# Seven block products in one more batch, all folds in one batch, and an order without a table of shifts

## The chip, the cores and the metric

The kernel runs on one core of a Trainium2 chip. The metric is the device time of one execution, in microseconds; less is better.

## The reference

Attention with a memory of 32 slots, then a two-layer perceptron with a squared ReLU, all in fp32:

```python
a = softmax(phi, axis=sequence)                  # phi: 8 batches, 8 heads, 576 x 32
k_m = einsum('bhsm,bhsd->bhmd', a, k)            # 32 x 64 for each head
v_m = einsum('bhsm,bhsd->bhmd', a, v)
attn = softmax(q @ k_m.T / 8, axis=slots) @ v_m  # 576 x 64 for each head
x = attn, with heads joined                      # 4608 x 512
h = x @ w_in                                     # 512 x 2048
g = relu(h) ** 2
out = g @ w_out                                  # 2048 x 512
```

## The kernel before, in words

**Products.** Each fp32 operand of a large product is split into a rounded part and a rest (hi and lo), and three matmuls stand for one: hi x hi, hi x lo, lo x hi. v_m is never multiplied with the attention weights: it is folded into w_in beforehand (vw_alone, vw_step and vw_quad), so that the first product of the perceptron takes the attention weights (ath, atl: 256 x 576 for a batch) and a folded w_in (tiles vw).

**Stages.** memory(b, hh), a "unit", makes k_m and v_m of four heads of a batch. attention(b) makes scores (psc, line 840), the softmax (lines 949 to 955) and the turned weights at, ath and atl (lines 971 to 975). Then a batch has 16 steps, one for each 128 columns of w_in: mm1(g) (line 1013, into the banks h, then relu and square into gh and glo) and mm2(g) (lines 1044, 1045, 1047, into four banks acc, 512 columns each, one for each 128 tokens). g counts steps: batch b, from 2 on, has 16b to 16b + 15. The last 64 tokens of each batch go into tiles gl, and are multiplied for two batches at once (mm2_left, accl, line 1279).

**Folds of batches 4 to 7.** vw_quad(s, hh) folds one piece of w_in for all four batches at once: twelve matmuls into the banks pv and pa (pvq, line 784), ScalarE's cast (line 412, the line of the helper that copies), VectorE's subtraction (line 791), and POOL's store to DRAM (vw_kept, line 794). All use one buffer, named fold. Eight pieces s, two halves hh each; WHEN says after which steps of batches 3 and 4 a piece is recorded. vw_again loads the folded tiles back (line 805).

**Seven block products.** In batches from FAST on, fast(b, t, s) replaces mm1 and mm2: two steps' blocks of g (2 x 2 blocks with the 128-token blocks) and w_out are combined into sums, so that seven products of 256 columns do the work of eight. Its mm1 is line 1151, the sums are made on VectorE (lines 1171 to 1174), split into tiles H (ScalarE, line 1179) and LA, LB (VectorE, line 1180), and multiplied at lines 1208, 1209 and 1211 into banks Ma to Md. combine(s) turns w_out in place into the sums that these products need, during the batch before FAST. fast_left is what mm2_left is for these batches.

**What sets the order.** Every instruction is recorded as an Op of Plan with a cost and its dependences. Plan.order derives a due time for each and runs a list scheduler forward (and backward for due times), some twenty times; each engine takes the ready op with the smallest key. Before the last run a table, MOVED, shifts keys: a task (an invocation of a function, cut into pieces of 12 ops by named, begin and PART) gets its number times 100 ns added. TensorE's queue then runs in the order so found; where no op is ready for long in the first part, filled puts in filler matmuls.

Of the kernel before, what the change touches and what calls it, by code (L numbers as in the profile page):

```python
# [48 lines left out]
}  # L49
# [1425 lines left out]
```

## Time and profile before

| what | value |
| --- | --- |
| three runs | 762.48, 765.95, 766.16 us (median 765.95) |
| the profiled execution | 761.47 us, its span 759.4 us |
| TensorE's granted clock | 0.999 |
| busy: TensorE, VectorE, ScalarE | 739.4, 606.0, 414.0 us |
| DMA | 135.62 MB, mean 179 GB/s |

Steps begin at 44.0 us (batch 0), 248.3 (batch 2), 331.1 (batch 3), 437.2 (batch 4), 522.7 (batch 5), 592.8 (batch 6) and 670.7 (batch 7). The span goes from the first to the last instruction, and the time of an execution is about 2 us more. PE is TensorE, PEld its weight loads (beside the matmuls), DVE is VectorE, ACT is ScalarE. Records of neighbouring matmuls overlap, so what one costs is read from rows of several in a row, not from its own length. The granted clock of 0.999 is the upper of TensorE's two levels, 2.4 GHz, all the time.

### The profile page before, as it was taken

To read this page: it belongs to the slowest core of one execution; us is meant where nothing else is said; L and a number is where in the kernel's file an instruction comes from. 1 tells how busy PE (TensorE), PEld (TensorE's weight loads), DVE (VectorE), ACT (ScalarE), POOL (GpSimd) and SP (SyncE) were. 2 spreads that over 40 slices of the span, in tenths; PEclk is the share of its full clock that TensorE was granted. 3 is DMA by queue.
4 is the path that set the end of the run, shared out by engine and by line. 5 is a ranking of instruction groups with operands and counts; after the bars stand their busy time and mean duration, and the time that the engine had idled before them with its cause. 6 is when DMAs were issued, how large, how long until landed. Compare 5 with 4: busy or idle time off the path is not lost.

```text
span 759.4 us, 14838 instructions
## 1 busy us (share of the span) xinstructions
PE 739.4 (97%) x5392; PEld 648.5 (85%) x5392; DVE 606.0 (80%) x1410; ACT 414.0 (55%) x928; POOL 77.8 (10%) x133
## 2 busy tenths in 40 slices
PE   4999999999999999999999999999999999999997
PEld 3687889888787888888888888888888999999997
DVE  4899999996679799867478546578999878987984
ACT  3577788875462565633344223435675745755561
POOL 4112221110100100001101211101000100000000
PEclk9999999999999999999999999999999999999999
DMA  9998996667755947634667878764310345445421
GB/s 268 315 303 227 286 288 202 190 193 201 212 144 170 249 135 208 189 107 122 220 203 247 267 201 273 257 181 106 110 32 0 90 115 149 139 131 160 137 76 42
DMA packets 82632, 135.62 MB, mean 179 GB/s; under 512 B 26080, under 2 KB 52704, under 8 KB 82560
## 3 DMA queue, kind: packets, MB, share of 16 engines
q1 hardware_dynamic: 67168, 98.40, 44.9%
q0 software_dynamic: 15296, 36.15, 15.9%
q8 instruction: 43, 0.70, 0.4%
q14 instruction: 29, 0.24, 0.1%
q10 hardware_dynamic: 96, 0.13, 0.1%
HBM read 96.14 MB, written 34.80 MB: 172 GB/s over the span
## 4 chain that ended last, share of the span: by engine, by line
PE 84%; DVE 7%; DMA 5%; issue 2%; ACT 1%; SPq 1%; POOL 0%; DVEq 0%; POOLq 0%; ACTq 0%
PE h L1013 18%; PE acc L1047 11%; PE acc L1044 11%; PE acc L1045 11%; PE h L1151 6%; PE accl L1263 3%; PE psc L840 3%; PE accl L1279 3%; PE pkv L622 2%; PE pvw L754 2%; PE pvq_pv L784 2%; DMA vw<-vw_kept 1%; DVE work L500 1%; PE Mc L1211 1%; DMA wi<-w_in_kept 1%
## 5 line engine op out<-in xcount | busy, mean ns | idle before, releaser
L1013 PE MATMUL h<-ath,vw 128*128 128x256 f32 (+1 forms) x768 | 157.5, 301 | 0.0
L1044 PE MATMUL acc<-wo,gh 128*128 128x512 f32 x384 | 155.1, 404 | 0.0
L1045 PE MATMUL acc<-wo,gh 128*128 128x512 f32 x384 | 150.9, 393 | 0.0
L1013 PEld LDWEIGHTS h<-ath,vw 128*128 128x128 f32 x768 | 124.9, 189 | 10.2 <-ACT r L1017 0.7
L1047 PE MATMUL acc<-wo,glo 128*128 128x512 f32 x384 | 127.4, 402 | 0.0
L1017 ACT ACTIVATE r<-h 128x320 f32<-128x320 f32 (+1 forms) x136 | 54.2, 406 | 61.5 <-PE h L1013 56.3
L1019 ACT ACTIVATE gh<-r 128x512 fp32r<-128x512 f32 x96 | 60.6, 632 | 45.2 <-DVE r L1018 23.3
L1044 PEld LDWEIGHTS acc<-wo,gh 128*128 128x128 f32 x384 | 72.3, 188 | 14.3 <-issue 0.4
L1047 PEld LDWEIGHTS acc<-wo,glo 128*128 128x128 f32 x384 | 70.7, 188 | 16.0 <-issue 0.8
L1045 PEld LDWEIGHTS acc<-wo,gh 128*128 128x128 f32 x384 | 72.3, 188 | 12.5
L1013 PE MATMUL h<-atl,vw 128*128 128x256 f32 (+1 forms) x384 | 82.4, 295 | 0.1
L1023 DVE TENSOR_TENSOR glo<-r,gh 128x512 fp32r<-128x512 f32 x96 | 65.7, 685 | 15.3 <-PE acc L1047 8.0
L1013 PEld LDWEIGHTS h<-atl,vw 128*128 128x128 f32 x384 | 61.6, 189 | 0.5 <-DVE atl L935 0.3
L1021 ACT ACTIVATE r<-r 128x576 f32<-128x576 f32 x77 | 52.7, 684 | 1.8
L1151 PE MATMUL h<-ath,vw 128*128 128x256 f32 (+1 forms) x256 | 52.9, 299 | 0.4 <-DMA vw<-vw_kept 0.3
L412 ACT CAST vw<-pvw 64x512 fp32r<-64x512 f32 (+1 forms) x64 | 37.1, 580 | 22.7 <-PE pvw L754 16.9
L1018 DVE TENSOR_SCALAR r<-h 128x320 f32<-128x320 f32 (+1 forms) x56 | 25.6, 457 | 27.4 <-PE h L1013 26.6
L1151 PEld LDWEIGHTS h<-ath,vw 128*128 128x128 f32 x256 | 39.8, 188 | 1.5 <-issue 0.7
L762 DVE TENSOR_TENSOR vw<-pvw,vw 64x512 fp32r<-64x512 f32 x48 | 33.0, 687 | 4.5 <-ACT vw L412 3.6
L794 POOL DMA_DIRECT2D vw_kept<-fold x32 | 17.3, 540 | 108.0 <-DVE fold L791 100.2
L598 DVE TENSOR_REDUCE mx<-phi 128x128 f32<-128x640 f32 x16 | 21.1, 1316 | 8.7 <-DMA phi<-in_phi_dram 6.4
L840 PE MATMUL psc<-qT,kb 128*128 128x256 f32 (+1 forms) x96 | 27.4, 407 | 0.3 <-DVE qT L835 0.3
(254 smaller groups left out, 1614.4 us busy)
## 6 DMA issues: line engine op xcount, KB each, us to landing
vw<-vw_kept SPq DMA_DIRECT2D x192, 128.0 KB, 4.3
wi<-w_in_kept SPq DMA_DIRECT2D x40, 512.0 KB, 4.8
vw_kept<-fold POOLq DMA_DIRECT2D x32, 512.0 KB, 4.2
KV<-in_v_dram SPq DMA_DIRECT2D x16, 512.0 KB, 6.4
...
```

Of the source, the lines that this page charges most:

```text
L412: nc.scalar.copy(o, i) if e == "ACT" else ENG[e].tensor_copy(o, i)
L762: vec({"DVE": 700}, lambda e, part=part, pr=pr: nc.vector.tensor_sub(part(1), pw()[pr], part(0).bitcast(F32)), [pw, (V, (0, hf))], [(V, (1 ...
L840: nc.tensor.matmul(pq()[:, 0:32 * n], kb()[:, x].rearrange("p h m -> p (h m)"), qT()[:, x, 0:n].rearrange("p c t -> p (c t)"), start=(x == ...
L1013: nc.tensor.matmul(p()[:, 0:n], V()[:, l, hh, c0:c0 + P], x()[:, hh, cs], start=(i == 0), stop=(i == 5))
L1017: op({"ACT": act(n) - 40, **({} if b < 2 else {"DVE": tt(n)})}, lambda e, cs=cs, n=n, p=p: nc.scalar.activation(r()[:, cs], p()[:, 0:n], A ...
L1019: op({"ACT": act(SM)}, lambda e: nc.scalar.activation(gh(), r()[:, 0:SM], AF.Square), [r], [gh])
L1021: op({"ACT": act(S), **({} if b < 2 or b == FAST - 1 else {"DVE": tt(S)})}, lambda e: nc.scalar.activation(r(), r(), AF.Square) if e == "A ...
L1023: vec({"DVE": tt(SM)}, lambda e: nc.vector.tensor_sub(glo(), r()[:, 0:SM], gh().bitcast(F32)), [r, gh], [glo])
L1044: nc.tensor.matmul(a(), gh()[:, c], t()[:, 0], start=f0, stop=False)
L1045: nc.tensor.matmul(a(), gh()[:, c], t()[:, 1], start=False, stop=False)
L1047: nc.tensor.matmul(a(), glo()[:, c], t()[:, 0], start=False, stop=f1)
L1151: nc.tensor.matmul(p()[:, at:at + n], V()[:, l, hh, f0:f0 + P], x()[:, hh, cs], start=(i == 0), stop=(i == 5))
```

## The change

Batch 5 is done with seven block products too (FAST 6 to 5), so combine runs in batch 4. All eight pieces of the folds of batches 4 to 7 are recorded in batch 3, and none in batch 4. The units of batches 4 to 7 come earlier: seven in batch 2 and one in batch 3, where there were four and four. The second half of each fold goes into two buffers of the tag vw0. The table of shifts is removed, with what numbered its tasks. The buffers for the last ordinary batch's output come in another order.

```diff
-PART = 12
-MOVED = {
-    1: -263, 2: -101, 6: 20, 10: 21, 18: 27, 20: 61, 22: -57, 28: -6, 32: 388, 36: 21, 42: 15, 52: -266, 54: 53,
...
-}
...
-    def begin(self):
...
-    def named(self, fn):
...
-        if self.steps == PART:
-            self.begin()
-        self.steps += 1
         o = Op()
-        o.task = self.task
...
-        moved = [k + 100 * MOVED.get(o.task, 0) for k, o in zip(best[1], self.ops)]
-        self.forward(moved)
+        self.forward(best[1])
...
-    FAST = 6
+    FAST = 5
...
-    @plan.named
     def decode(kind, j, h, room):
...
-    WHEN = (8, 10, 12, 14), (0, 3, 6, 9)
-
-    @plan.named
+    WHEN = (3,5,6,8,9,11,13,15),()
+
     def vw_quad(s, hh):
 
         if not room:
             room.append(st([P, 2, 2, 2, SL], F32R, "KV", "fold"))
-        Z = room[0]
+        if hh:
+            Z = [(st([P, 2, 2, SL], F32R, "vw0", f"fold{s}_{g}", 2), None) for g in (0, 1)]
+        else:
+            Z = [(room[0], g) for g in (0, 1)]
...
         for g in (0, 1):
-            part = lambda l, g=g: Z()[:, g, l].rearrange("p x f -> p (x f)")
...
+            z, i = Z[g]
+            view = lambda z=z, i=i: z() if i is None else z()[:, i]
+            part = lambda l, view=view: view()[:, l].rearrange("p x f -> p (x f)")
...
         if b == FAST - 1:
-            return [(st([P, DM], F32, x, f"o{b}_{i}", n), None) for i, (x, n) in enumerate((("r", 2), ("r", 2), ("qT", 1), ("S", 2)))]
+            return [(st([P, DM], F32, x, f"o{b}_{i}", n), None) for i, (x, n) in enumerate((("qT", 1), ("S", 2), ("r", 2), ("r", 2)))]
...
+    ready = []
+
     def quad(s):
...
-        if s in (1, 2, 6, 7):
+        if s in (0, 1, 2, 3, 5, 6, 7):
             units(1)
     for ff in range(NFF):
         step(pos[3, ff])
-        if ff < 8 and ff % 2 == 0:
+        if ff in (0,):
             units(1)
         if ff in WHEN[0]:
             quad(WHEN[0].index(ff))
...
-            if b == FAST - 1 and ff % 2:
-                combine(ff // 2)
+            if b == FAST - 1 and ff % 2 and (b > QUAD or ff > max(WHEN[1], default=-1)):
+                for s in range(len(ready), ff // 2 + 1):
+                    ready.append(combine(s))
```

Behind the cut, line numbers are lower by 40 to 52: line 784 becomes 740, 791 becomes 749, 840 becomes 796, 1013 becomes 966, 1023 becomes 976, 1044 and 1045 become 996 and 997, 1180 becomes 1130, 1279 becomes 1227.

**TensorE, the last score product of batch 4** (psc4_1_1; acc3 and gh58 or gh63 are mm2 of batch 3; accl3 is mm2_left). Before, it stood in step 58:

```order
L1044 MATMUL acc3_0_0_4347<-wo50_1609,gh58_4837 128x512
L1045 MATMUL acc3_0_0_4347<-wo50_1609,gh58_4837 128x512
L840 MATMUL psc4_1_1_4869<-qT4_1_1_4853,kb4_1_3577 128x320 x2
L1044 MATMUL acc3_0_1_4354<-wo50_1609,gh58_4837 128x512
L1045 MATMUL acc3_0_1_4354<-wo50_1609,gh58_4837 128x512
```

Now it stands in step 63, and mm2_left and the last folds follow it:

```order
L996 MATMUL acc3_0_3_4356<-wo71_2099,gh63_5189 128x512
L997 MATMUL acc3_0_3_4356<-wo71_2099,gh63_5189 128x512
L796 MATMUL psc4_1_1_5296<-qT4_1_1_5282,kb4_1_3901 128x320 x2
L1227 MATMUL accl3_5231<-wo51_1661,gl2_5_3961 128x512 x3
L1227 MATMUL accl3_5231<-wo60_1916,gl2_6_4052 128x512 x3
L740 MATMUL pvq6_0_pv_5312<-wi2_6_0_5024,VTh21_3028 128x256
```

And at the end of this stretch, the last rows of the last half fold and the first matmuls of batch 4 (h64_0):

```order
L740 MATMUL pvq7_0_pa_5393<-wi2_7_0_5159,VTh21_3028 128x256
L740 MATMUL pvq7_0_pv_5391<-wi2_7_0_5159,VTl21_3038 128x256
L740 MATMUL pvq7_0_pa_5393<-wi2_7_0_5159,VTl21_3038 128x256
L966 MATMUL h64_0_5409<-ath4_5259,vw4_0_4564 128x256 x2
L966 MATMUL h64_0_5409<-atl4_5264,vw4_0_4564 128x256 x2
```

Before, five steps of batch 3 and six half folds stood between; now 18 matmuls of 512 columns and three half folds.

**VectorE, the same place: what it does from the copy of batch 3's output (o3) to atl4, the operand of h64_0.** S4_1 is the score tile of batch 4's second half, fold the tiles of vw_quad. Now:

```order
L371 COPY o3_0_5221<-acc3_0_1_4346 128x512
L749 TENSOR_TENSOR fold_4492<-pvq6_0_pv_5312,fold_4492 128x512
L907 TENSOR_REDUCE rz4_1_None_5344<-S4_1_5289 128x18
L749 TENSOR_TENSOR fold_4492<-pvq6_0_pa_5314,fold_4492 128x512
L908 TENSOR_SCALAR rz4_1_None_5344<-rz4_1_None_5344 128x18
L791 STREAM_TRANSPOSE qT5_0_0_5356<-q5_0_5291 128x2x256
L909 RECIPROCAL rz4_1_None_5344<-rz4_1_None_5344 128x18
L910 TENSOR_TENSOR S4_1_5289<-S4_1_5289,rz4_1_None_5344 128x576
L925 STREAM_TRANSPOSE at4_1_0_5380<-S4_1_5289 128x256
L749 TENSOR_TENSOR fold6_0_5378<-pvq6_1_pv_5360,fold6_0_5378 128x512
L749 TENSOR_TENSOR fold6_1_5382<-pvq6_1_pa_5362,fold6_1_5382 128x512
L929 TENSOR_TENSOR atl4_5264<-at4_1_0_5380,ath4_5259 128x256
```

Before, the same softmax stood among the steps of batch 3 (r60, glo59 further on):

```order
L844 STREAM_TRANSPOSE S4_1_4857<-psc4_1_1_4869 128x320
L828 TENSOR_TENSOR kb5_1_4883<-kTa5_1_3816,bd_72 128x256
L949 TENSOR_REDUCE red4_1_None_4887<-S4_1_4857 128x18
L950 TENSOR_TENSOR S4_1_4857<-S4_1_4857,red4_1_None_4887 128x576
L791 TENSOR_TENSOR fold_4535<-pvq2_0_pa_4893,fold_4535 128x512
L791 TENSOR_TENSOR fold_4535<-pvq2_0_pv_4891,fold_4535 128x512
L952 TENSOR_REDUCE rz4_1_None_4932<-S4_1_4857 128x18
L835 STREAM_TRANSPOSE qT5_0_0_4951<-q5_0_4860 128x2x256
L953 TENSOR_SCALAR rz4_1_None_4932<-rz4_1_None_4932 128x18
L954 RECIPROCAL rz4_1_None_4932<-rz4_1_None_4932 128x18
L955 TENSOR_TENSOR S4_1_4857<-S4_1_4857,rz4_1_None_4932 128x576
L1018 TENSOR_SCALAR r60_4977<-h60_1_4957 128x320
```

Ahead of the piece of now stand the same four instructions with which the piece of before begins (lines 844 to 950 there).

**VectorE, the start of batch 5** (glo79 is the last subtraction of batch 4's steps). Now, with the last pieces of combine (wo, T, E, F) and the sums of the first products (X, XD, LA):

```order
L976 TENSOR_TENSOR glo79_6273<-r79_6209,gh79_6243 128x512
L1046 TENSOR_TENSOR wo61_1900<-E6_1_6239,wo61_1900 128x256
L1046 TENSOR_TENSOR T6_6271<-F6_6041,T6_6271 128x512
L1051 TENSOR_TENSOR E7_1_6292<-F7_6198 128x256 x2
L1121 TENSOR_TENSOR X80_6252<-X80_6252,XD_6280 128x256
L1122 TENSOR_TENSOR X80_6252<-XD_6280,X80_6252 128x128
L1046 TENSOR_TENSOR wo70_2177<-E7_1_6292,wo70_2177 128x256
L1123 TENSOR_TENSOR XD_6280<-X80_6252 128x128
L1046 TENSOR_TENSOR wo71_2099<-E7_1_6292,wo71_2099 128x256
L1124 TENSOR_TENSOR XD_6280<-XD_6280 128x128
L1105 TENSOR_SCALAR X81_6324<-h81_0_6245 128x256
L1052 TENSOR_TENSOR F7_6198<-F7_6198 128x512
```

Before, with the output of batch 4 (o4) and ordinary steps (r80, r81, glo80):

```order
L1023 TENSOR_TENSOR glo79_6127<-r79_6083,gh79_6108 128x512
L971 STREAM_TRANSPOSE at5_1_1_6132<-S5_1_5984 128x320
L1024 TENSOR_TENSOR gl4_7_6062<-r79_6083,gl4_7_6062 128x64
L975 TENSOR_TENSOR atl5_5997<-at5_1_1_6132,ath5_5994 128x320
L412 COPY o4_0_6145<-acc4_0_0_5346 128x512
L412 COPY o4_1_6153<-acc4_0_2_5353 128x512
L835 STREAM_TRANSPOSE qT6_0_1_6165<-q6_0_5986 128x640
L844 STREAM_TRANSPOSE S6_0_6177<-psc6_0_0_6150 128x256
L1018 TENSOR_SCALAR r80_6174<-h80_1_6167 128x320
L1018 TENSOR_SCALAR r81_6196<-h81_0_6181 128x256
L844 STREAM_TRANSPOSE S6_0_6177<-psc6_0_1_6191 128x320
L1023 TENSOR_TENSOR glo80_6208<-r80_6174,gh80_6194 128x512
```

In the first steps of the program the order differs too: on VectorE, ahead of glo6, the subtraction of step 6, stand seven more instructions than before, and ahead of glo7 nine fewer.

## Rows read from the trace of the kernel before

**Rows 1.** The profile's page, its part 1: busy time of each engine, its share of the span, and instructions.
```profile
PE 739.4 (97%) x5392; PEld 648.5 (85%) x5392; DVE 606.0 (80%) x1410; ACT 414.0 (55%) x928; POOL 77.8 (10%) x133
```

**Rows 2.** Waits of TensorE between 183 and 760 us: who waited at which line, for whom: us in total, times, longest. The answer has one more row, of 0.2 us.
```profile
PE h L1151 <- DMA vw<-vw_kept: 0.3, 1, 0.3
PE psc L840 <- DVE qT L835: 0.3, 1, 0.3
...
```

**Rows 3.** Busy time in three stretches: first half of batch 0, batch 5, batch 6. Columns: us, then busy us (x instructions) of PE, of PE's weight loads, of DVE, ACT and POOL, granted clock, DMA share, GB/s.
```profile
44.00:101.90 57.90, 55.27 (x450) 46.77 (x449) 57.19 (x129) 45.28 (x99) 11.84 (x14) 1.00 0.92 270
522.70:592.80 70.10, 70.10 (x386) 61.66 (x385) 64.36 (x148) 45.12 (x105) 2.59 (x4) 1.00 0.22 55
592.80:670.70 77.90, 77.30 (x596) 75.36 (x595) 66.16 (x192) 47.65 (x118) 4.01 (x6) 1.00 0.50 134
```

**Rows 4.** The chain of waits, in order of time: start us, us, what. Rows of 512 columns (L1279), 256 (the first L1151, and L1263) and 320 (the second L1151).
```profile
233.37 4.15 PE accl L1279 x18
...
592.97 1.42 PE h L1151 x12
...
652.85 1.76 PE h L1151 x12
...
744.90 10.03 PE accl L1263 x84
```

**Rows 5.** Timeline of TensorE around one half of a fold of batches 4 to 7 (twelve matmuls of L784): start us, us, what. First matmul of it, and what follows it.
```profile
363.55 0.38 PE L784 MATMUL pvq_pv<-wi,VTh 64*128 64x256 f32 x1
...
364.45 0.50 PE L1013 MATMUL h<-ath,vw 128*128 128x256 f32 x2
```

**Rows 6.** Groups of VectorE's instructions, shapes apart: line, operation, out<-in, out<-in (partitions x elements), count | busy us, mean ns of one | idle us ahead of them. In the order in which the prediction adds them up.
```profile
L844 DVE STREAM_TRANSPOSE S<-psc 128x320 f32<-128x320 f32 x12 | 6.2, 513 | 3.6 <-PE psc L840 3.4
L828 DVE TENSOR_TENSOR kb<-kTa,bd 128x256 f32<-128x256 f32 x6 | 2.4, 394 | 0.0
L949 DVE TENSOR_REDUCE red_None<-S 128x18 f32<-128x576 f32 x12 | 9.0, 748 | 0.0
L950 DVE TENSOR_TENSOR S<-S,red_None 128x576 f32<-128x576 f32 x12 | 9.0, 751 | 0.2
L412 DVE COPY o<-acc 128x512 f32<-128x512 f32 x12 | 8.0, 688 | 2.5 <-PE acc L1047 2.2
L791 DVE TENSOR_TENSOR fold<-pvq_pv,fold 128x512 fp32r<-128x512 f32 x16 | 10.8, 678 | 1.4 <-ACT fold L412 1.4
L952 DVE TENSOR_REDUCE rz_None<-S 128x18 f32<-128x576 f32 x12 | 8.9, 742 | 1.2 <-ACT S L951 1.1
L791 DVE TENSOR_TENSOR fold<-pvq_pa,fold 128x512 fp32r<-128x512 f32 x16 | 11.0, 686 | 10.5 <-ACT fold L412 10.5
L953 DVE TENSOR_SCALAR rz_None<-rz_None 128x18 f32<-128x18 f32 x12 | 1.9, 162 | 0.1
L835 DVE STREAM_TRANSPOSE qT<-q 128x512 f32<-128x512 f32 x12 | 8.4, 701 | 2.1 <-DMA q<-in_q_dram 2.1
L954 DVE RECIPROCAL rz_None<-rz_None 128x18 f32<-128x18 f32 x12 | 3.2, 263 | 0.3
L955 DVE TENSOR_TENSOR S<-S,rz_None 128x576 f32<-128x576 f32 x12 | 9.1, 756 | 0.2
L971 DVE STREAM_TRANSPOSE at<-S 128x256 f32<-128x256 f32 x12 | 5.2, 437 | 0.1
L975 DVE TENSOR_TENSOR atl<-at,ath 128x256 fp32r<-128x256 f32 x12 | 5.0, 420 | 0.2
```

**Rows 7.** Timeline of VectorE at two neighbours: start us, us, what.
```profile
12.89 0.41 DVE L497 TENSOR_SCALAR work<-raw 128x512 f32<-128x512 f32 x1
13.23 0.42 DVE L499 TENSOR_SCALAR work<-raw 128x512 uint32<-128x512 uint32 x1
```

**Rows 8.** Busy time of the score matmuls alone (line 840), batch 5: us, PE busy (x records), PEld busy, granted clock, DMA share, GB/s.
```profile
522.70:592.80 70.10, 3.87 (x14) 2.08 (x12) 1.00 0.22 55
```

**Rows 9.** Waits of VectorE in batch 6 (592.8 to 670.7 us): us in total, times, longest.
```profile
DVE XD L1155 <- PE h L1151: 1.8, 4, 0.9
DVE qT L835 <- DMA q<-in_q_dram: 1.7, 1, 1.7
DVE LA L1180 <- ACT S L951: 1.2, 1, 1.2
DVE X L1171 <- ACT XD L1169: 0.8, 2, 0.5
```

**Rows 10.** Groups of VectorE's instructions, as in rows 6: two of the six passes that decode a weight piece.
```profile
L500 DVE SCALAR_TENSOR_TENSOR work<-work 128x512 uint32<-128x512 uint32 x32 | 22.0, 686 | 1.5 <-ACT work L498 1.4
L497 DVE TENSOR_SCALAR work<-raw 128x512 f32<-128x512 f32 x32 | 13.4, 419 | 1.0 <-DMA raw<-in_moe_w_in_dram 0.8
```

**Rows 11.** Busy time from the first to the last fold matmul, and in ten microseconds of it. Columns as in rows 3.
```profile
363.60:491.80 128.20, 128.20 (x771) 108.14 (x772) 75.69 (x151) 48.35 (x104) 20.41 (x36) 1.00 0.76 242
472.00:482.00 10.00, 10.00 (x68) 8.92 (x67) 5.58 (x12) 3.74 (x9) 1.59 (x3) 1.00 0.87 284
```

**Rows 12.** The tile of the folds: what its instructions' engine sat idle for, us and times. This one is ScalarE's cast, that waits for the store before.
```profile
  DMA vw_kept<-fold: 23.0, 12
```

**Rows 13.** A stretch of batch 7 (columns as in rows 3), and one group of weight loads (columns as in rows 6).
```profile
701.60:743.00 41.40, 41.40 (x329) 41.40 (x328) 36.42 (x119) 24.52 (x63) 0.00 (x0) 1.00 0.35 103
L1208 PEld LDWEIGHTS Ma<-wo,H 128*128 128x128 f32 x64 | 12.1, 189 | 0.0
```

More of the change, by code (lines that the diff above doesn't have):

```diff
@@ L76 @@
 class Op:
-    __slots__ = ("ways", "fn", "deps", "users", "late", "cap", "left", "ready", "count", "start", "end", "lead", "size", "seq", "lat", "banks", "cold", "boost", "task", "uses")
+    __slots__ = ("ways", "fn", "deps", "users", "late", "cap", "left", "ready", "count", "start", "end", "lead", "size", "seq", "lat", "banks", "cold", "boost", "uses")
 class Plan:
@@ L90, in __init__ @@
         self.count = {}
-        self.tasks = self.task = 0
-        self.steps = 0
     def buf(self, tag, make, n=1):
@@ L102, in buf @@
         return b
-    def begin(self):
-        self.tasks += 1
-        self.task, self.steps = self.tasks, 0
-    def named(self, fn):
-        def run(*args, **more):
-            self.begin()
-            got = fn(*args, **more)
-            self.begin()
-            return got
-        return run
     def op(self, ways, fn, r=(), w=(), lead=False, cap=None, size=(), lat=None, cold=None, boost=0):
-        if self.steps == PART:
-            self.begin()
-        self.steps += 1
         o = Op()
-        o.task = self.task
         o.ways, o.fn, o.lead, o.cap, o.size, o.lat, o.cold, o.boost = ways, fn, lead, cap, size, lat, cold, boost
@@ L722, in vw_alloc @@
             VW[2 * n + bp, s] = st([P, 2, 2, SL], F32R, tag, f"vw{n}_{bp}_{s}", bufs)
-    @plan.named
     def vw_alone(s, bp):
@@ L743, in vw_alone @@
         op({"ACT": acp(2 * SL)}, lambda e: copy(e, part(1), pw()), [pw], [(V, 1)], lead=True)
-    @plan.named
     def vw_step(n, s, hh):
@@ L766, in tile_attention_moe @@
     room = []
-    WHEN = (8, 10, 12, 14), (0, 3, 6, 9)
-    @plan.named
+    WHEN = (3,5,6,8,9,11,13,15),()
     def vw_quad(s, hh):
@@ L788, in vw_quad @@
         for g in (0, 1):
-            part = lambda l, g=g: Z()[:, g, l].rearrange("p x f -> p (x f)")
-            op({"ACT": acp(2 * SL)}, lambda e, part=part, g=g: copy(e, part(0), pw[g]()), [pw[g]], [(Z, (g, 0))], lead=True)
+            z, i = Z[g]
+            view = lambda z=z, i=i: z() if i is None else z()[:, i]
+            part = lambda l, view=view: view()[:, l].rearrange("p x f -> p (x f)")
+            op({"ACT": acp(2 * SL)}, lambda e, part=part, g=g: copy(e, part(0), pw[g]()), [pw[g]], [(z, (g, 0))], lead=True)
             vec({"DVE": tt(2 * SL)}, lambda e, part=part, g=g: nc.vector.tensor_sub(part(1), pw[g](), part(0).bitcast(F32)),
-                [pw[g], (Z, (g, 0))], [(Z, (g, 1))], lead=True)
+                [pw[g], (z, (g, 0))], [(z, (g, 1))], lead=True)
             at = 4 * s + 2 * hh + g
-            dma(lambda d, g=g, at=at: d(w_folded()[at * P:(at + 1) * P, :], Z()[:, g].rearrange("p l x f -> p (l x f)").bitcast(F32)), [(4096 * P, 4096)],
-                r=[(Z, (g, 0)), (Z, (g, 1))], w=[(w_folded, at)], eng="POOL", lead=True)
-    @plan.named
+            dma(lambda d, view=view, at=at: d(w_folded()[at * P:(at + 1) * P, :], view().rearrange("p l x f -> p (l x f)").bitcast(F32)), [(4096 * P, 4096)],
+                r=[(z, (g, 0)), (z, (g, 1))], w=[(w_folded, at)], eng="POOL", lead=True)
     def vw_again(b, s, t=None):
@@ L809, in tile_attention_moe @@
     att = {}
-    @plan.named
     def scores(b, hh, split):
@@ L852, in scores @@
         return s_t
-    @plan.named
     def first_attention(b):
@@ L991, in left_part @@
         return gl[s][1]
-    @plan.named
     def mm1(g):
@@ L1025, in mm1 @@
         gt[g] = gh, glo
-    @plan.named
     def mm2(g):
@@ L1062, in tile_attention_moe @@
     T = {}
-    @plan.named
     def combine(s):
@@ L1122, in ring @@
         return pt("pv", name) if turns[0] % 5 == 1 else pt("acc", name, 4)
-    @plan.named
     def fast(b, t, s):
@@ L1236, in fast @@
                 store_rows(o, o, [(b, 4 * (2 * t + x) + c) for c in range(4)])
-    @plan.named
     def fast_left(b, g):
@@ L1268, in fast_left @@
         evac(a, (o, None), lambda: o(), [(b - 1, 16), (b - 1, 17), (b, 16), (b, 17)])
-    @plan.named
     def mm2_left(b, g):
```

2 lines of the change are left out of this document (removed), and 15 rows, old and new, of the table MOVED.

## The prediction

> **What bounds the kernel now.** I read the page's busy shares first: TensorE is busy for 97% of the span, VectorE for 80%, ScalarE for 55% [rows 1]. A share of 97% leaves two questions: where the other 3% lies, and whether another engine sets TensorE's pace anywhere. The waits answer the first: from 183 us on TensorE has three waits, none over 0.3 us [rows 2]. The stages answer the second [rows 3]: at 44 to 101.9 us (first half of batch 0) VectorE is busy for 57.19 of 57.90 us and TensorE loses 2.6; in batch 5, still in the ordinary form, TensorE is busy for all of 70.10 us; in batch 6, in the form of seven block products, it has 77.30 of 77.90, with VectorE at 66.16. So behind the first stage the time is the sum of TensorE's instructions, and a change pays by the columns it takes out of TensorE's queue, as long as TensorE gets no new wait. The chain of waits prices those columns: 18 matmuls of 512 columns take 4.15 us, 0.2306 each; 12 of 256 columns 1.42 us, 0.118; 84 in a row 10.03 us, 0.119; 12 of 320 columns 1.76 us, 0.147 [rows 4].
>
> **Batch 5 in seven block products: -4.5 us.** Counted from the instructions: 192 matmuls of 512 columns leave mm2 (64 on each of its three lines) and 336 of 256 columns come in fast (seven products x 3 x 16). mm1 keeps its 192 matmuls of the same widths, and fast_left and mm2_left run as often as before. -192 x 0.2306 + 336 x 0.1183 = -44.3 + 39.8 = -4.5. All of it lies on the path, since TensorE is the bound there.
>
> **The step from batch 3 to batch 4: +2 us (0 to 4).** All folds now stand in batch 3, and attention(4) comes late among them. By the order, before, the last score product of batch 4 (psc4_1_1) had five steps of batch 3 and six half folds behind it, some 36 us of TensorE's work ahead of h64_0, the first matmul group of batch 4. Now 18 matmuls of 512 columns and three half folds stand there: 4.15 us [rows 4] and 3 x 0.90 (twelve matmuls from 363.55 to 364.45 us) [rows 5], 6.85 in all. Against that VectorE must finish sixteen instructions until atl4, the operand of h64_0. From the rows by form: 0.513 + 0.394 + 0.748 + 0.751 + 0.688 + 0.678 + 0.742 + 0.686 + 0.162 + 0.701 + 0.263 + 0.756 + 0.437 + 0.678 + 0.686 + 0.420 = 9.30 us [rows 6]. Neighbours overlap by 0.07 (12.89 + 0.41 against a start at 13.23) [rows 7], so 15 x 0.07 less: 8.25. In it ScalarE's exponential lies beside the copy of o3 and a fold. And the last half fold itself, 0.90, needs the banks that VectorE empties as its next to last instruction, at about 7.9: it ends at 8.8. So h64_0 starts some 8.8 - 6.85 = 2 us late; nothing else can go in front of it, since TensorE's queue is in order. Taken: 2. Bounds: 0 if ScalarE takes over quicker than counted, 4 if VectorE also stands still three times for as long as one of its subtractions (0.69), for ScalarE's casts of the folds.
>
> **VectorE in the new batch 5: +1.5 us (0 to 4).** Between glo79 and LA95 VectorE has 195 instructions. Batch 6 now runs 192 in 66.16 us busy [rows 3], 0.345 each, so 67.2. TensorE's work of the same stretch: 96 x 0.118 + 96 x 0.147 + 336 x 0.118 = 65.1 and about 3 for the scores (3.87 where records that overlap are merged, in the like stretch [rows 8]): 68.1. Two engines at 67.2 and 68.1 cannot both stay without waits: VectorE waits in batch 6 for TensorE, ScalarE and loads 1.8, 1.7, 1.2 and 0.8 us [rows 9], hidden there by 11.4 us of fast_left's matmuls that batch 5 does not have. Low end: none of it shows; high end: 67.2 + 5.5 - 68.1 = 4.6, held to 4 as some of it is at the seams. I take 1.5, near the low end, because in batch 6 TensorE lost only 0.6.
>
> combine, which turns w_out into the sums for the products, goes from batch 5 to batch 4, same instructions; TensorE is not in it, and batch 4 loses the folds' casts and subtractions, so VectorE has room there. Cost 0; its last pieces (wo70, wo71, F7) stand among the first instructions of batch 5, and this is a part of the 1.5.
>
> **The order without the table: +1 us (-2 to +3).** Without the table of shifts the first steps differ. Ahead of glo6 VectorE has seven more instructions, six of them decoding: 3 x 0.686 + 3 x 0.419 + 0.2 = 3.5 us [rows 10], in a stretch where VectorE is busy all the time [rows 3]; ahead of glo7 nine fewer, and ahead of glo13 as many as before. What is late at glo6 is so made up at glo7, unless TensorE ran dry between: at most 3. Low end -2: the nine fewer serve TensorE earlier. Later batches have no such place; units of batch 2 move by one or two steps, under TensorE at 100%, cost 0.
>
> **The folds' transfers: +1 us (0 to 6.4).** Before, the folds lay over 363.6 to 491.8 us, 128.2 us with 242 GB/s at a DMA share of 0.76 [rows 11]: 31.0 MB. Now between the first and the last stand 36 fewer matmuls of 256 columns, 30 fewer of 320 and 100 fewer of 512: 31.8 us less, so 96.4. The 32 stores and 13 reloads of 0.524 MB stay (23.6 MB); the rest, 7.4 MB, shrinks with the stretch to 5.6. 29.2 MB in 96.4 us are 303 GB/s. Full use would be 242 / 0.76 = 318; the best ten microseconds of before had 284 at 0.87 [rows 11]. At 284 it takes 102.8: +6.4; at 318 nothing. I take 1, as these transfers have slack of whole steps on both ends. For it speaks also the second change to the folds: with one buffer the next fold waited for the store, 23.0 us in 12 waits on ScalarE [rows 12]; two more buffers take these away. That alone is worth 0, since TensorE did not wait for it.
>
> **The sum.** -4.5 + 2 + 1.5 + 1 + 1 = +1.0 against the profiled execution's 761.47: 762.5. That execution lies 0.6% below the median of the three runs, 765.95; moved by the same 1.0, the median gives **767 us**. A measurement of this kernel can tell about 0.5%, 3.8 us, from no change, so the forecast is no change.
>
> **Rivals.**
> A, all waits are absorbed: the queue ahead of h64_0 and VectorE's seams have more slack than counted. For it: no wait over 0.3 us now [rows 2]. Against: 6.85 against 8.8 us leaves no slack. Gain 4.5: 761.4.
> B, the transfers bound the folds, slower than before: 29.2 MB at 284 GB/s end 6.4 us late, and with them the last folds and h64_0. It decides from the point at which batch 3 asks for more than 284 GB/s over the whole stretch; 303 is asked. 767 - 1 + 6.4 = 772.4; with all 31.0 MB in the stretch, 109.2 us, 12.8 late: 778.8. Against: a rate of 0.87 was seen while the stores waited for one buffer, so it need not be a ceiling.
> C, VectorE bounds batch 5 with its waits: the high end of that term and some of it again at combine's last pieces, 767 - 1.5 + 5.5 = 771.
> D, weight loads stay in view. The 144 additional matmuls (336 - 192) bring 144 loads of 128x128. In 701.6 to 743 us, with products of 256 columns, TensorE and its loads are both busy for all of 41.40 us, and a load takes 189 ns, more than the 118 from matmul to matmul [rows 13]: loads run beside matmuls, so the price is 0. If each came in the open, 144 x 0.189 = 27 us: 794.
> The Trainium skill, "TensorE: Matmul & The Clock Gate", Part 3 ("What overlaps and what doesn't"), has a rule against this change: a load overlaps with running matmuls only when it goes to other rows of the array; these loads use all 128 rows, as the matmuls do. By that rule D would hold; the trace disagrees, 41.40 and 41.40 of 41.40 us.
> E, the order is worse in many places: the table had moved 176 pieces of work, and with it TensorE had next to no wait. Without it 40 waits of the 0.3 us that is the longest now [rows 2] are 12 us: 779. Against: VectorE's slack outside the first stage and batches 5 to 7.
>
> **Numbers.** Forecast 0.40, A 0.22, B 0.15, C 0.13, E 0.08, D 0.02. Faster by over 0.5% (under 762.1) is A's larger part, 0.20; within 0.5% the forecast and A's rest, 0.42; slower (over 769.8) are B to E, 0.38. The range of 758 to 778 takes A with the spread of the runs (762.48 to 766.16) at the low end, and B and C at the high end; D and most of E stay out.
>
> **What would show it.** In the profile after: TensorE's matmuls of the products 336 more, and busy time about 4.5 less; a wait of h64_0 for atl4 of 1 to 3 us (the second term; none means A); in batch 5 waits of products for VectorE's LA and L tiles of 1 to 4 us in sum (C if over 4); a DMA share above 0.9 between the folds and a wait for wi or vw tiles (B); losses in the first 140 us (the table). Wrong altogether would be a time of batch 5 that is not 3 to 5 us shorter against its ordinary form with the same attention beside it, or waits spread over batches 2 to 4 that no term names.

## The result: 0.7% slower, by waits that the products' gain does not cover

| | runs | median, us | lowest to highest |
| --- | --- | --- | --- |
| before | 13 | 764.22 | 760.58 to 766.86 |
| changed | 13 | 769.40 | 766.05 to 773.05 |

The ratio is 1.0067, 95% interval 1.0042 to 1.0091: 5.1 us slower (3.2 to 7.0). The forecast was +1.0 and no measurable change. The time lies in the range of 758 to 778. Taken by itself, 769.40 is still in the band that stood for no change (762.1 to 769.8, chance 0.42); but before came out at 764.22 and not at 765.95, so the ratio is over 0.5%, on the slower side, which had 0.38. The profiled execution of the changed kernel took 767.19 us, its span 765.4.

**Where it went.** The page of the changed kernel, engines' busy time, against [rows 1]:

```profile
PE 737.0 (96%) x5533; PEld 652.9 (85%) x5533; DVE 618.9 (81%) x1494; ACT 429.2 (56%) x984; POOL 79.9 (10%) x133
```

TensorE has 2.4 us less to do by its records, and the span is 6 us longer. Its waits from 150 us on, against [rows 2] (us in total, times, longest):

```profile
PE pvq_pv L740 <- DVE fold L749: 1.7, 1, 1.7
PE Mb L1158 <- ACT H L1129: 1.4, 2, 0.9
PE pvt L646 <- DVE kvn L632: 1.1, 1, 1.1
PE pvw L708 <- DVE vw L716: 0.7, 1, 0.7
PE h L966 <- ACT r L970: 0.7, 2, 0.5
PE pmx L556 <- DVE mx L554: 0.5, 1, 0.5
PE pvq_pa L740 <- DVE fold L749: 0.2, 1, 0.2
```

Before, there were three waits of 0.3 us at most in the same stretch. The list holds 6.3 us, but many small delays never become a row, as records overlap. So I worked out a **loss**: the time at which the first matmul of a step starts, less the work that TensorE has in front of it, each matmul at the usual spacing of its kind (0.231, 0.118 and 0.147 us for 512, 256 and 320 columns, for the others their spacing in the trace of before, nothing for fillers). It is good for comparing kernels at the same place, and each row comes from one execution: in the first stages two executions of one order differ by 3 to 4 us (e10 and e11 below). In us, at the first matmul of batch 2, of steps 60, 68 and 76 (late batch 3, early and late batch 4), of batch 6, and at the last matmul; the last column is all of TensorE's work at the usual spacings:

```
                      batch 2   60     68     76    batch 6  end    work
before                 36.0    42.9   43.9   45.3   46.5    49.6   705.0
changed                39.6    47.0   53.8   54.2   57.1    60.1   700.3
e1 scores early        39.8    47.4   49.1   50.6   77.5    79.5   700.3
e2 one buffer          40.5    47.8   60.4   60.7   68.0    70.9   700.3
e3 both seams          39.6    49.8   53.8   54.7   77.3    80.8   700.3
e4 no table            44.1    54.5   61.4   62.4   65.0    69.2   705.0
e5 first table         58.7    67.4   73.9   74.3   77.7    81.1   700.3
e6 five normal         40.1    48.0   54.1   54.6   56.3    60.8   705.0
e7 seam alone          39.8    47.2   50.8   51.7   54.6    57.4   705.0
e8 products alone      40.1    49.8   52.5   53.1   64.9    67.3   700.3
e9 seams free          38.4    46.7   48.8   49.5   54.8    56.6   700.3
e10 table first        39.8    47.0   51.6   56.7   62.1    66.2   705.0
e11 table rest         39.9    48.2   49.4   50.8   51.9    55.0   705.0
e12 seams free 2       39.0    45.6   47.7   48.9   52.1    55.7   700.3
```

The work falls from 705.0 to 700.3 us, -4.7. That is a count at usual spacings, not a measurement; that the products do run at this spacing shows in the loss, which grows by only 2.9 us from step 76 to batch 6, with 321 of their matmuls in batch 5. What is measured apart, by e6 below, is 5.4 us by the profiles. The loss is 10.5 larger: 3.6 of it up to batch 2, 5.8 between steps 60 and 68, 1.7 between step 76 and batch 6, little elsewhere.

**The seam between batches 3 and 4.** TensorE's timeline (start us, us, what): the end of the second to last half fold that stands in front of h64_0, the last one in front of it, and the first groups of batch 4 (one more half fold follows later, up to 466.9 us).

```profile
450.34 0.28 PE L740 MATMUL pvq_pa<-wi,VTl 64*128 64x256 f32 x1
452.27 0.38 PE L740 MATMUL pvq_pv<-wi,VTh 64*128 64x256 f32 x1 [1.65 <-DVE fold L749]
452.87 0.39 PE L740 MATMUL pvq_pa<-wi,VTh 64*128 64x256 f32 x1 [0.22 <-DVE fold L749]
...
453.77 0.51 PE L966 MATMUL h<-ath,vw 128*128 128x256 f32 x2
...
455.29 0.80 PE L966 MATMUL h<-ath,vw 128*128 128x256 f32 x2 [0.47 <-ACT r L970]
```

And VectorE's, first and last of the sixteen instructions that the prediction counted, with the one that waited:

```profile
444.26 0.52 DVE L800 STREAM_TRANSPOSE S<-psc 128x320 f32<-128x320 f32 x1 [2.00 <-PE psc L796]
...
446.98 0.69 DVE L371 COPY o<-acc 128x512 f32<-128x512 f32 x1 [0.45 <-PE acc L999]
...
451.57 0.65 DVE L749 TENSOR_TENSOR fold<-pvq_pv,fold 128x512 fp32r<-128x512 f32 x1
452.14 0.67 DVE L749 TENSOR_TENSOR fold<-pvq_pa,fold 128x512 fp32r<-128x512 f32 x1
452.74 0.41 DVE L929 TENSOR_TENSOR atl<-at,ath 128x256 fp32r<-128x256 f32 x1
```

The sixteen took 444.26 to 453.15 us, 8.9 (8.25 were counted, and the copy's wait of 0.45 explains most of the rest). mm2_left's matmuls begin at 443.82, so h64_0 was due 6.85 later, at 450.67, and came at 453.77: 3.1 late instead of 2. The mechanism is the one predicted, down to the half fold in front of h64_0 that waits for a bank; the sign that I had given, a wait of h64_0 itself for atl4, did not appear, since that half fold took the wait (1.65 and 0.22 us). Not predicted is what follows. TensorE's busy time and granted clock in single microseconds there (us, PE busy, PEld, DVE, ACT, POOL, granted clock, DMA share, GB/s):

```profile
450.00:451.00 1.00, 0.62 (x11) 0.41 (x7) 0.97 (x3) 0.54 (x2) 1.00 (x2) 1.00 1.04 242
451.00:452.00 1.00, 0.00 (x0) 0.00 (x0) 0.96 (x3) 0.96 (x3) 0.48 (x2) 1.00 0.77 201
452.00:453.00 1.00, 0.51 (x3) 0.31 (x5) 1.00 (x3) 0.08 (x1) 1.00 (x2) 1.00 0.80 206
...
454.00:455.00 1.00, 0.82 (x6) 0.54 (x5) 0.93 (x3) 0.15 (x1) 0.00 (x0) 0.77 0.94 181
455.00:456.00 1.00, 0.71 (x3) 0.71 (x4) 0.93 (x3) 0.24 (x1) 0.00 (x0) 0.50 0.73 205
456.00:457.00 1.00, 1.00 (x6) 1.00 (x6) 0.04 (x2) 0.00 (x0) 0.37 (x1) 0.50 0.92 217
457.00:458.00 1.00, 1.00 (x5) 1.00 (x5) 0.40 (x1) 0.00 (x0) 0.19 (x1) 0.53 0.87 213
458.00:459.00 1.00, 1.00 (x9) 0.82 (x7) 0.28 (x1) 0.90 (x2) 0.00 (x0) 1.00 0.86 223
```

Some 2 us behind the wait the granted clock fell to 0.5, the lower of the two levels (1.2 GHz), for some 3.5 us: 0.23 + 0.50 + 0.50 + 0.47 = 1.7 us of full clock lost. With 3.1 late and the wait of 0.47 at h65 that makes most of the 5.8.

**Batches 5 and 6, and the folds.** Busy time by stage of the changed kernel: batch 5 and batch 6, answering to [rows 3], the stretch from the first to the last fold matmul, VectorE while combine runs in batch 4, and, answering to [rows 11] like the third line, 20 us of the folds.

```profile
528.10:601.20 73.10, 72.46 (x555) 70.48 (x555) 69.37 (x207) 49.66 (x126) 4.14 (x6) 1.00 0.56 154
601.20:680.80 79.60, 78.69 (x625) 77.63 (x624) 67.32 (x199) 42.60 (x107) 2.68 (x4) 1.00 0.47 129
```
```profile
365.10:466.90 101.80, 99.39 (x615) 82.69 (x614) 61.66 (x118) 39.09 (x84) 20.32 (x36) 0.98 0.81 273
481.00:531.00 50.00, 50.00 (x276) 43.82 (x275) 50.00 (x118) 33.79 (x84) 0.00 (x0) 1.00 0.15 36
```
```profile
380.00:400.00 20.00, 20.00 (x130) 16.60 (x130) 10.96 (x22) 8.13 (x20) 4.01 (x8) 1.00 1.00 363
```

TensorE stays nearly full in batch 5. In these 20 us of the folds 363 GB/s were moved with TensorE at 20.00 of 20.00: neither the 284 that I had as a possible ceiling nor the 318 that I had as full use was one. (The trace of before, too, has 320 GB/s, between 20 and 40 us.) And VectorE is busy for all of the 50 us in which it makes combine's sums. ScalarE's waits for the fold buffers, 23.0 us in [rows 12], are down to this (us, times):

```profile
  DMA vw_kept<-fold: 4.4, 2
```

### The profile page after: what moved, and what is told of

It is laid out like the page before. It is cut to its first block, busy times and chain, and to the rows that moved or that the text cites. A ratio compares the mean times of both kernels' runs of the same rounds, so it can differ in the third digit from the quotient of the medians.

```text
span 765.4 us, 15298 instructions
## 1 busy us (share of the span) xinstructions
PE 737.0 (96%) x5533; PEld 652.9 (85%) x5533; DVE 618.9 (81%) x1494; ACT 429.2 (56%) x984; POOL 79.9 (10%) x133
## 3 DMA queue, kind: packets, MB, share of 16 engines
q0 software_dynamic: 15296, 36.15, 15.1%
## 4 chain that ended last, share of the span: by engine, by line
PE 56%; issue 17%; DVE 10%; DMA 9%; POOL 3%; ACT 3%; SPq 2%; POOLq 0%; ACTq 0%; DVEq 0%
PE h L1101 9%; PE h L966 8%; PE acc L999 5%; PE acc L997 5%; PE acc L996 5%; PE psc L796 2%; PE accl L1212 2%; DMA wo<-work 2%; PE pkv L578 2%; POOL vw_kept L752 2%; PE Mb L1158 2%; PE accl L1227 2%; PE Mb L1159 1%; PE Ma L1158 1%; PE Ma L1159 1%
## 5 line engine op out<-in xcount | busy, mean ns | idle before, releaser
L966 PE MATMUL h<-ath,vw 128*128 128x320 f32 (+1 forms) x640 | 134.5, 301 | 0.8 <-ACT r L970 0.7
L996 PE MATMUL acc<-wo,gh 128*128 128x512 f32 x320 | 130.7, 408 | 0.0
L997 PE MATMUL acc<-wo,gh 128*128 128x512 f32 x320 | 125.9, 393 | 1.3 <-DMA wo<-work 1.3
L999 PE MATMUL acc<-wo,glo 128*128 128x512 f32 x320 | 96.7, 403 | 0.7 <-DVE glo L976 0.7
L970 ACT ACTIVATE r<-h 128x256 f32<-128x256 f32 (+1 forms) x128 | 51.0, 409 | 71.7 <-PE h L966 66.5
L1101 PE MATMUL h<-ath,vw 128*128 128x256 f32 (+1 forms) x384 | 78.7, 296 | 0.0
L996 PEld LDWEIGHTS acc<-wo,gh 128*128 128x128 f32 x320 | 60.3, 188 | 13.5 <-issue 1.2
L997 PEld LDWEIGHTS acc<-wo,gh 128*128 128x128 f32 x320 | 60.2, 188 | 11.6 <-DMA wo<-work 1.6
L966 PE MATMUL h<-atl,vw 128*128 128x256 f32 (+1 forms) x320 | 68.8, 297 | 0.0
L966 PEld LDWEIGHTS h<-atl,vw 128*128 128x128 f32 x320 | 51.7, 190 | 0.0
L1129 ACT CAST H<-X 128x512 fp32r<-128x512 f32 x48 | 29.7, 619 | 24.3 <-DVE X L1122 24.0
L1101 PE MATMUL h<-atl,vw 128*128 128x256 f32 (+1 forms) x192 | 40.9, 294 | 0.0
L1130 DVE TENSOR_TENSOR LA<-X,H 128x512 fp32r<-128x512 f32 x48 | 32.6, 679 | 3.5 <-ACT H L1129 3.4
L1101 PEld LDWEIGHTS h<-atl,vw 128*128 128x128 f32 x192 | 30.8, 188 | 0.0
```

The lines of the kernel that those rows point to most:

```text
L966: nc.tensor.matmul(p()[:, 0:n], V()[:, l, hh, c0:c0 + P], x()[:, hh, cs], start=(i == 0), stop=(i == 5))
L970: op({"ACT": act(n) - 40, **({} if b < 2 else {"DVE": tt(n)})}, lambda e, cs=cs, n=n, p=p: nc.scalar.activation(r()[:, cs], p()[:, 0:n], A ...
L996: nc.tensor.matmul(a(), gh()[:, c], t()[:, 0], start=f0, stop=False)
L997: nc.tensor.matmul(a(), gh()[:, c], t()[:, 1], start=False, stop=False)
L999: nc.tensor.matmul(a(), glo()[:, c], t()[:, 0], start=False, stop=f1)
L1101: nc.tensor.matmul(p()[:, at:at + n], V()[:, l, hh, f0:f0 + P], x()[:, hh, cs], start=(i == 0), stop=(i == 5))
```

## The experiments

Each was timed against the kernel before on the same chip; ratios are to it, with 95% intervals. Diffs are against the changed kernel where nothing else is said.

**e1: attention(4) recorded earlier.**

```diff
-        if ff == 11:
+        if ff == 5:
             attention(4)
```

> The changed kernel with attention(4) recorded at step 5 of batch 3 instead of step 11 (behind two folds instead of six). By the order 24.8 us of TensorE work now stand between the last score product of batch 4 and h64_0 (6.9 in the changed kernel), but in batch 5 only 9.7 us against some 22 us of VectorE's work, as combine gathers there. Theory S (a seam costs what VectorE has more than TensorE between the last score product and the first matmul of the next batch, and the clock falls behind it): no wait and a clock of 1.00 at the start of batch 4, a wait of 8 to 14 us at the start of batch 5 with the clock under 1.00 behind it; time 770 to 780. Rival D (the folds' transfers cost the time, not the order at the seam): the loss at batch 4 stays, nothing new at batch 5; time 768 to 771.

Measured: 785.07 us, ratio 1.0256 (1.0228 to 1.0283). The seam at batch 4 was gone (loss from step 60 to 68 1.7, against 6.8), and a larger one stood at batch 5. TensorE's waits between 500 and 560 us, and two stretches (columns as above):

```profile
PE h L966 <- ACT r L970: 7.4, 1, 7.4
PE acc L999 <- DVE glo L976: 5.4, 1, 5.4
PE psc L796 <- DVE S L800: 3.4, 1, 3.4
...
```
```profile
440.00:460.00 20.00, 20.00 (x122) 17.22 (x121) 8.62 (x17) 9.56 (x20) 5.77 (x9) 1.00 0.93 291
...
520.00:540.00 20.00, 7.21 (x16) 4.53 (x16) 20.00 (x47) 7.66 (x18) 0.00 (x0) 0.59 0.07 18
```

Theory S holds in kind and is too small in size: from step 76 to batch 6 the loss is 26.9 us (2.9 in the changed kernel), and the time lies beyond what I gave. VectorE was idle for more than half of 440 to 460 us and full behind 520. The first of combine's additions stands at 505.58 us, behind the last fold (its subtraction at 499); in the changed kernel these are 480.55 and 472.57, and in between lies the last fold's store, issued at 474.5 with a median of 5.6 us to its landing: 480.1. By the code, combine's tiles F share the buffers vw0 with the folds, so it cannot begin before the folds have been stored; no addition is seen to wait for a store, it is the plan that puts them behind it. e2, where the folds leave vw0 alone, shows the other case (combine's additions, first and last start; the changed kernel and then e2):

```profile
L1038 DVE TENSOR_TENSOR F<-wo x16: 669/677/683, 480.5 to 525.7; 128x512 f32<-128x512 f32 x16
L1038 DVE TENSOR_TENSOR F<-wo x16: 630/686/694, 360.5 to 536.1; 128x512 f32<-128x512 f32 x16
```

The edit also moved the folds: their matmuls lie at 383.4 to 495.5 us, in the changed kernel at 365.1 to 466.8. By the code the place of attention(4) behind six folds pulls these forward: its scores take the bank pa after them, so they inherit its due time.

**e2: one fold buffer.**

```diff
-        if hh:
+        if False:
             Z = [(st([P, 2, 2, SL], F32R, "vw0", f"fold{s}_{g}", 2), None) for g in (0, 1)]
```

> The changed kernel with the single fold buffer of before. By the order 1.8 us of TensorE work against 5.9 of VectorE's stand at the start of batch 4, and 10.6 against 11.4 at batch 5. Theory S: a wait of 4 to 6 us at batch 4, a longer dip of the clock, a short wait at batch 5; time 771 to 775. Rival D: the folds wait for their stores again (20 us on ScalarE), the last folds come later, and TensorE stands between the folds; time 775 or more. If the two buffers are worth nothing: 769.

Measured: 778.79 us, 1.0175 (1.0146 to 1.0204). ScalarE's wait for the store, and TensorE's longest wait between 440 and 470 us:

```profile
  DMA vw_kept<-fold: 18.8, 11
```
```profile
PE pvq_pv L740 <- issue: 3.0, 1, 3.0
```

The two buffers are worth 8 us in the changed kernel (1.0175 against 1.0067), where I had put them at nothing. The time and the signs are those that I had given to Rival D: the folds wait for their stores, and TensorE stands at a fold. The clock at half, from 456.5 us for 6.8 us, is Theory S's sign. That the folds' transfers are not what the changed kernel loses by is shown by e9 and e12 below, where the folds end 6 to 8 us earlier and the seam is free. In e2 the last fold came at 507 us instead of 473, in the middle of batch 4; 5.8 us more loss stand between steps 60 and 68, 4.4 from step 76 to batch 6.

**e3: attention(4) at step 8, attention(5) with more priority.** A number of ns (`o.boost = boost + self.extra`) that is taken off an op's key, so that the plan places it earlier, set around attention(5):

```diff
-        if ff == 11:
+        if ff == 8:
             attention(4)
...
             if ff == 9:
+                plan.extra = 30000
                 attention(b + 1)
+                plan.extra = 0
```

> The changed kernel with attention(4) recorded at step 8 of batch 3 (behind four folds) and attention(5)'s instructions given 30 us more priority. By the order 9.4 us of TensorE work against 7.7 of VectorE's at batch 4, 15.2 against 8.5 at batch 5. Theory S: no wait over 0.5 us at either seam, the clock 1.00 throughout, 5 us less than the changed kernel: 764 to 765. Rival T (most of the loss is the table's, spread over the first stages): 768 to 769. Rival D: 767 or more.

Measured: 786.30 us, 1.0277 (1.0244 to 1.0310). Between steps 60 and 68 the loss was 4.0 (6.8 in the changed kernel); from step 76 to batch 6 it was 22.6 (2.9), with this wait:

```profile
PE acc L1000 <- DVE glo L977: 14.3, 1, 14.3
```

My expectation failed: I had counted only what stands between a score product and the next batch's first matmul. With combine late (first addition at 502 us), VectorE has all of it left in the last third of batch 4, and whatever has priority over it, something else waits: here the rest of batch 4's own steps.

**e4: the kernel before, with an empty table.** `MOVED = {}`, against before.

> The kernel before with an empty table of shifts, all else as before (six ordinary batches, folds and units in their old places). Theory T (the table is worth some 4 us in batches 0 and 1): 768 to 769, with TensorE losing 2 us up to the second half of batch 0, 3.6 us by the start of batch 2, and little behind it. Rival (the losses in the first stages come from the units and folds that moved, which look forward in the plan): 764 to 765. My prediction's term was 1 us.

Measured: 780.76 us, 1.0200 (1.0171 to 1.0229): 15 us. In the place of before the table was worth far more than I had thought, 8.1 us of loss by batch 2, and 5.9 between steps 60 and 68 (6.9 against 1.0), where this wait stood:

```profile
PE pvq_pv L767 <- issue: 3.9, 1, 3.9
```

Neither theory had the size. Against a kernel without the table, the rest of the change is thus some 10 us faster (1.0067 against 1.0200), where my terms had the rest at 0 (-4.5 + 2 + 1.5 + 1): what the table is worth on the old order and what the rest of the change is worth on the new one were both off, in opposite directions.

**e5: the first 60 entries of the table on the changed kernel.**

```diff
+MOVED = {
+    1: -263, 2: -101, 6: 20, 10: 21, 18: 27, 20: 61, 22: -57, 28: -6, 32: 388, 36: 21, 42: 15, 52: -266,
...
+        moved = [k + 100 * MOVED.get(o.task, 0) for k, o in zip(best[1], self.ops)]
```

> The changed kernel with the first 60 entries of the table put back, those of the tasks ahead of batch 2's steps. Theory T (the table is worth 3.6 us there, as the losses of the two traces say, 39.6 us against 36.0 at the first matmul of batch 2): loss of about 36 us at that place, the seam at batch 4 as in the changed kernel: 765 to 766.5. Rival (the entries fit only the order they were found for): 769 to 771.

Measured: 789.30 us, 1.0325 (1.0296 to 1.0355). The rival held in kind, with some 19 us more than it said: TensorE waits 11.8 us for folds of the first batches, and within the longer of the two waits the granted clock falls to half.

```profile
PE pvw L743 <- DVE vw L751: 11.8, 2, 7.9
...
```
```profile
120.00:140.00 20.00, 12.08 (x59) 10.55 (x59) 17.62 (x35) 13.70 (x29) 3.72 (x4) 0.74 0.71 204
```

By the code the shifts are relative to keys of the plan that they were found on; on the keys of this one they do harm.

**e6: batch 5 ordinary again.** `FAST = 6`, all else as changed.

> The changed kernel with batch 5 ordinary again (combine in batch 5, folds and units in their new places, two more buffers, no table). Theory P (the products are worth 4.7 us of TensorE's work and cost 1.7 us of waits at the start of batch 5): 3 us slower than the changed kernel, 772 to 774. Rival U (combine in batch 4 costs as much as the products give): 768 to 770.

**e7: e6 with attention(4) at step 8.**

```diff
-        if ff == 11:
+        if ff == 8:
             attention(4)
```

> The kernel of e6 with attention(4) recorded at step 8 of batch 3 instead of 11; there is no combine in batch 4 here that could gather. By the order 9.9 us of TensorE work against 8.1 of VectorE's at batch 4 (6.4 against 7.7 in e6), 16.8 against 7.5 at batch 5. Theory S: the wait at batch 4 and the dip of the clock go, 4 to 6 us less than e6: 767 to 769. Rival: the wait appears elsewhere, within 1 us of e6.

Measured: e6 775.17 us, 1.0155 (1.0115 to 1.0195); e7 769.93, 1.0068 (1.0043 to 1.0092). e6 against the changed kernel gives the products in this place: 0.9% (some 7 us, with a wide interval) by the runs, 5.4 by the ends of the two profiles. That is no less than the 4.7 of work, so combine in batch 4 costs next to nothing once the folds end early; Rival U does not hold, Theory P does in kind, 1 us beyond its times. e7 against e6 is the seam with no product in it: 5 us by the runs, 3.3 by the ends of the two profiles, of which 2.5 lie between steps 60 and 68. Its edit moves the folds too (matmuls at 381.8 to 487.9 us, in e6 at 365.2 to 464.8). TensorE at the seam, e6 and then e7:

```profile
440.00:460.00 20.00, 17.48 (x105) 13.57 (x104) 12.99 (x27) 5.22 (x11) 5.76 (x9) 1.00 0.60 156
```
```profile
440.00:460.00 20.00, 19.41 (x118) 15.87 (x119) 14.64 (x29) 10.03 (x22) 6.96 (x11) 1.00 0.82 253
```

In this execution of e6 TensorE stood still there for as long in all as in the changed kernel (17.48 us busy, 17.59 there), but in waits of 0.8 us at most, and the clock stayed at 1.00.

**e8: the products alone.** Against e4: `FAST = 5`, combine recorded in batch 4, the buffers of the output in the other order; folds half in batch 4, units in their old places, one fold buffer.

> The kernel without table (e4) with seven block products in batch 5 as the only further change: folds half in batch 4, units in their old places, one fold buffer. Theory C (combine cannot begin before the last folds have given up its buffers and VectorE has to do all of it in the last third of batch 4): the first of combine's additions only behind the last fold, at some 500 us, a wait of 10 us or more at the start of batch 5 with the clock at half behind it, 788 to 800, slower than e4's 780.8 in spite of the products. Rival P (the products give their 4.7 us wherever the folds are): 776.

Measured: 777.06 us, 1.0164 (1.0133 to 1.0195). Nearly the time of Rival P, and Theory C's mechanism in part. Its sign failed: with one fold buffer, which is not in vw0, combine's first four additions stand at 362 to 370 us, ahead of nearly all folds. But the fifth comes at 493 us only, the last fold's subtraction at 508, and the rest of combine falls into the last third of batch 4. Between step 76 and batch 6 TensorE loses 11.8 us (2.6 in e4), this wait among them, and a clock that falls to half within it, at 526.4 us, for 6.8 us:

```profile
PE acc L999 <- DVE glo L976: 4.4, 1, 4.4
```

That it is not slower than e4 (0.4% faster, within the intervals) is because e4 lost 6.9 between steps 60 and 68 and e8 only 2.7, and e4 lost 4 more ahead of batch 2: the order came out otherwise. e8 is so no clean measure of the products.

**e9 and e12: slack planned at both seams, no table.** The changed kernel, attention(4) at step 9, and priorities in us for units, folds, attention(4) and attention(5): 5, 20, 5, 10 in e9, 12, 25, 0, 10 in e12 (set around the calls as in e3).

> The changed kernel with other priorities, no table: attention(4) recorded at step 9 of batch 3 and 5 us earlier in the plan, attention(5) 10 us, the folds 20 us, the units 5 us. By the order both seams have slack: 14.7 us of TensorE work against 7.7 of VectorE's at batch 4, 32.6 against 9.0 at batch 5. Theory S: no wait over 0.7 us and a clock of 1.00 at both seams; of the changed kernel's 10.4 us of loss 5.8 at batch 4 and 1.7 at batch 5 go: 761.5 to 764.5. Rival F (folds and combine in one batch each are too much for VectorE or the transfers, whatever the seams): 768 or more, with new waits in batches 3 to 5.

> The kernel of e9 with the folds 25 us, the units 12 us and attention(4) 0 us earlier in the plan; slack at both seams again (11.9 against 7.7 us, 31.7 against 8.7). Theory S (what the changed kernel loses more than a kernel without waits at its seams is 5 us, whatever the rest of the order): 762 to 765, as e9, with no dip of the clock at batch 4. Rival (e9 was a lucky order, orders without a table differ by 5 us and more for other reasons): 768 or more.

Measured: e9 764.18 us, 0.9998 (0.9971 to 1.0025); e12 762.67, 0.9977 (0.9953 to 1.0001). Between steps 60 and 68 both lose 2.1 (6.8 in the changed kernel). TensorE at the place of the seam, e9 and then e12:

```profile
440.00:460.00 20.00, 20.00 (x134) 16.22 (x131) 13.19 (x27) 9.27 (x19) 7.46 (x12) 1.00 0.95 295
```
```profile
440.00:460.00 20.00, 20.00 (x129) 16.63 (x129) 13.43 (x28) 9.58 (x19) 7.94 (x13) 1.00 0.94 300
```

Theory S holds at batch 4: two orders with slack there both end 5 to 7 us under the changed kernel. The folds lie as close together as in the changed kernel, their matmuls at 364.5 to 458.7 us in e9 and to 460.5 in e12, and combine is in batch 4, so that folds and combine have one batch each is not what costs (Rival F). Both runs also moved units and folds, so the 5 to 7 us are not the seam's alone. At batch 5 nothing was gained: from step 76 to batch 6 e9 lost 5.3, e12 3.2, the changed kernel 2.9. e12 is the best of all, and level with before: its interval touches 1.

**e10 and e11: the two parts of the table.** The kernel before with the first 60 entries alone, and with the other 116 alone.

> The kernel before with only the first 60 entries of its table (the tasks ahead of batch 2's steps). TensorE's order is that of before up to there, and without table behind. If the trace of e4 splits its 15 us rightly (8.1 lost by the first matmul of batch 2, of it all in the part that these entries order): 772 to 773. Rival (the rest of the table is worth all of it, and early losses are caught up later): 779 or more.

> The kernel before without the first 60 entries of its table and with the other 116. TensorE's order behind batch 1 is that of before. If early losses are never caught up: 772 to 773, with 44 us of loss at the first matmul of batch 2 as in e4, and no more than before behind it. Rival (TensorE catches up, since later stages have slack): 766 or less.

Measured: e10 777.48 us, 1.0179 (1.0148 to 1.0210); e11 770.48, 1.0085 (1.0053 to 1.0116). The rest of the table is worth 14 us, the first entries 6; together more than the 15 of e4, so they do not add up. Neither time is one that I had given: e10 lies between its two, and e11 came out under the 772, with 39.9 us lost at batch 2 instead of 44. In e11 nothing is caught up later: 15.1 lost behind the start of batch 2, before 13.6. But the profiles of the first stages have a spread of their own. Up to step 28 TensorE's order in e10 is that of before, and at its first matmul e10 had lost 38.2, before 34.3; up to step 24 e11's is that of e4, with 36.5 and 39.5. Two executions of one order differ there by 3 to 4 us.

## Why the prediction was right and wrong

- **Bound.** Right: the time is TensorE's work and its waits. By the work alone it would have been 4.7 faster.
- **Products, -4.5.** Right: 5.4 by the profiles of e6 and the changed kernel, 0.9% by their runs. (The -4.7 of work is the same count again.) Rival D (loads in view) is out: 336 - 192 more loads came, 27 us if in the open, and the loss grew by 2.9 us from step 76 to batch 6.
- **The step from batch 3 to 4, +2 (0 to 4).** The mechanism was right, sixteen instructions against 6.85 us, and the step was mis-sized: 5.8 more loss than before. 3.1 came from the wait, for which I had left out that VectorE starts 0.44 us behind the first matmul of mm2_left (443.82 to 444.26, where the record of the last score matmul has just ended) and that it waits 0.45 us for the bank of o3; 1.7 from the clock behind the wait, for which there was no term; the rest from the groups that follow h64_0. e7, e9 and e12 gave this place slack and got back 5 us or more each by the runs, in three different orders; that the seam costs is shown, its exact share is not, since each of them moved other work with it.
- **Batch 5, +1.5.** Right in size: the loss from step 76 to batch 6 is 2.9, before 1.2, so +1.7. The sign that I had given, waits of the products for LA and L tiles of 1 to 4 us, is not there: between 528 and 602 us one wait of 0.5 us is listed, for ScalarE's H. The rest is spread over the steps, and what causes it is not shown. Rival C is out.
- **The order without the table, +1 (-2 to +3).** The loss ahead of batch 2 grew by 3.6, outside my bounds, at a place where I had argued from counts of instructions. How much of it is the order stays open, since one order gave 34.3 and 38.2 by step 28 in two executions. And the term as I put it, the table's worth, failed: in the place of before it is 15 us (e4). I priced a table by the places where two orders differ most, and took it that the rest has slack. Rival E, the one that priced the whole table, came near this (12 us), but its time of 779 is not that of this change.
- **The folds' transfers, +1 (0 to 6.4).** Too high: between the start of batch 2 and step 60, some 45 us into the folds, the changed kernel lost 7.4, before 6.9. Over all of the folds the DMA share was 0.81, with 363 GB/s in 20 us of them, and no wait of TensorE for a wi or vw tile from DRAM is listed. Rival B is out.
- **Two buffers, 0.** Wrong: 8 us (e2). I asked only who waits for the buffer now. With one buffer the folds end 35 us later, and both seams lose more. In e1 and e3 the loss at batch 5 comes with a combine that needs VectorE for some 50 us and begins late (at 506 and 502 us). In e2 its first four additions are early and it ends at 546 us instead of 537; that this is its loss at batch 5 is likely and not shown, and why the seam at batch 4 loses 5.8 more was not taken apart.
- **The likeliest case** was 5.5 us of waits against 4.5 of gain. Measured are 10.5 against 4.7: the sum was wrong by the seam (3.8) and the first stages (2.6), less 0.5 at the transfers and 1 in batch 4 (0.4 lost from step 68 to 76, before 1.4). Rival A is out with them. That the forecast came within 4 us is in part luck: two parts of the change that I had put at 1 and 0 us are worth 15 (the table, in the place of before) and 8 (the two buffers), and the rest of the change makes up for most of the first.
